# First q rows behind weights, two row blocks normalised together, last gates and Wo operands inside attention, two DMA queues at the end

## The chip, the cores and the metric

The kernel runs on one core of a Trainium2 chip. The metric is the device time of one execution in microseconds. The kernel before has a median of 1725.43 us over 3 runs (1724.54 to 1725.99). The core's engines run their own instruction streams in order and meet at semaphores: PE (TensorE, matrix products into PSUM), DVE (VectorE), ACT (ScalarE), POOL (GpSimd), and SP, which here only issues DMAs. Weight loads of PE are shown as PEld.

## The reference

The input x has 2048 rows of 512 numbers. Layer normalisation gives xn; attention with 32 heads of 16 numbers and a dense block with GELU both read it, and the second gates the first:

```python
x = A_x
xn = _layernorm(x, axis=-1)
# attention: qkv = xn @ wqkv; p = softmax(q k^T / 4); s = (p v) @ wo
s = _A_ref(xn, A_wqkv, A_wo)
# dense block: h = gelu(xn @ w1 + b1); h @ w2 + b2
g = _silu(_B_ref(xn, B_w1, B_b1, B_w2, B_b2))
return x + s * g
```

## The kernel before

Everything is float32. Products other than those of attention's probabilities are made from rounded halves: an operand is split into a part rounded to fp32r ("h", by ACT) and a remainder ("l", by DVE or POOL), and three matmuls (hh, hl, lh; `mm3`, L69) stand for one product.

*Stage 1 (L240 to L366)* walks over 16 blocks of 128 rows. For a block, `moments` (L267) takes the statistics on DVE, `rstd` (L272) makes one over the root with ACT's square root and four small DVE operations with a refinement, `norm` (L281) writes the normalised block and asks for a later block of x on SP, `turn` (L288) transposes it on PE and splits it (`split`, L65: ACT, then DVE), and `v_tile` (L296) multiplies it with the v weights, 12 matmuls. The v weights come in four pieces (`wv_r`), each rounded by ACT (L330) with its remainder by POOL (L331). SP asks for row blocks 0 and 1, then the four weight pieces, then row blocks 2 to 6. Twelve matmuls of an identity stand ahead of the first block (L325).

*Stage 2 (L476 to L507)* runs over 48 jobs: four make q and k rows for two groups of four heads each (`qk`), the other 44 are column blocks of the dense layer for a chunk of 512 rows (`up`, then `down` one job later). q and k go out to DRAM as halves (`qk_h`, `qk_l`) and come back in attention's layout: `load_k` (L96), `load_qs` (L127). The weights of a job (`raw`, two buffers) are asked for by `w_ahead` and split by `w_split` (ACT L236, POOL L237), both called in `behind`; on ACT the GELU of a job (L394, L395) stands behind the rounding of a later job's weights. Between the matmuls, `fill` puts score matmuls of attention's first pass (`s_one`, L158), each with a row maximum on DVE (L172). When one is due is set by a count of matmuls (slots) and by `LEAD`, how many are made in this stage (4 x 144), and `FILL0`, the slot from which they are spread (less 12).

*Stage 3 (L642 to L689)* is attention. 32 units (a group of four heads by a chunk of 512 queries) have 16 steps each; step n makes transposed scores on PE (`t_one`, L547), exp on ACT (L549) into one of three buffers, and the product with v one step behind (`pv_step`, L557). Other work is hung on a step and a place in it with `at(n, f, ..., pos=...)`: place 0 is behind the first of a step's four score matmuls and its exp, place 3, the usual one, behind the last. A unit's end is `o_move` (copy out of PSUM, denominators to `dr`, four row groups to `ot`), `o_den` (reciprocal, out to `den_d`, back as `dn`, spread over 16 partitions each) and `o_div` (L591, the division). When a chunk of queries has all its heads, its four row blocks get the product with Wo: `load_gx` (gate and x), `w_token` (operands split, L604, L605), `w_mul`, `w_out` (L622: multiply with the gate on DVE, add x, store). `gx` has four buffers, the split operands `oh` and `ol` three each.

*End (L690 to L706).* The last chunk's four row blocks (12 to 15; `T3`) are done by k instead of by block: `w_chunk(k)` splits 128 of the 512 columns for all four blocks, and the last column group alone waits for the last unit's division. The gates of these four blocks get their SiLU here; the others got theirs in stage 2.

The order of every engine is that of the program text. Every DMA from SP in the kernel before is issued in program order; a DMA issue also waits until the DMA that was issued eight before it has landed.

Of the kernel before, what the change touches and what calls it, by code (L numbers as in the profile page):

```python
# [10 lines left out]
AF = mybir.ActivationFunctionType  # L11
# [9 lines left out]
DH = 16  # L21
KT = D // P
NT = S // P
CH = 512
# [8 lines left out]
LEAD = 144  # L33
DONE = 490
KBACK = 71
FILL0 = 192
ORDER = {0: "TTTTV", 1: "TTTTSV", 2: "TTTSTSV", 3: "STTTSTSV", 4: "STTSTSVTS"}
KB = 3

# [2 lines left out]
def fused(ctx: ExitStack, tc: tile.TileContext, x, wqk, wv, wo, w1, b1, w2, b2, out):  # L42
    nc = tc.nc
# [13 lines left out]
    den_d = dpool.tile([NG * NCH, GH, CH], F32, name="den_d")  # L57
# [7 lines left out]
    def split(hi, lo, src):  # L65
        nc.scalar.activation(hi, src, AF.Copy)
        nc.vector.tensor_sub(lo, src, hi.bitcast(F32))  # L67
# [11 lines left out]
    NU = NG * NCH  # L79
# [23 lines left out]
    def k_zero(kt, i, eng):  # L103
        p, a = divmod(i, 2)
        eng.memset(kt[p][64 * a + 32:64 * a + 64].bitcast(F32), 0.0)

    def k_ones(kt):
        for p in range(2):
            for a in range(2):
                nc.sync.dma_start(kt[p][64 * a + 48:64 * a + 50].bitcast(F32), ones_d)  # L110
# [9 lines left out]
    def q_rows(qs, u):  # L120
        g, c = divmod(u, NCH)
        for a in range(2):
            for b, src in enumerate((qk_h, qk_l, qk_h)):
                r = 64 * a + DH * b
                nc.sync.dma_start(qs[a][r:r + DH].bitcast(F32), rows(src, g, 0, a, c * CH, CH))

    def load_qs(u):  # L127
        if u < LEAD // 16:
            QS[u] = qzs[u % 2]
            q_rows([QS[u][:, a] for a in range(2)], u)  # L130
        elif u < NU:
            QS[u] = qss[0][:, u % 2]
            q_rows([QS[u]] * 2, u)
# [106 lines left out]
    with ExitStack() as s1:  # L240
# [4 lines left out]
        def a_tile(shape):  # L245
            banks[0] += 1
            i = banks[0] % 6
            if i < 2:
                return ps_s.tile(list(shape), F32, name="ps")
            if i == 2:  # L250
                return ps_x.tile(list(shape), F32, name="ps")
            return ps_t.tile(list(shape), F32, name="pst")


        xs, xns = {}, {}

        def load_x(t):
            xs[t] = w1k.tile([P, D], F32, name="xt", bufs=7)
            nc.sync.dma_start(xs[t], x[t * P:(t + 1) * P, :])
# [7 lines left out]
        def moments(t):  # L267
            st = w1k.tile([P, 6], F32, name="st")
            nc.vector.bn_stats(st, xs[t])
            nc.vector.bn_aggr(mv[:, t, :], st)  # L270

        def rstd(t0, t1):  # L272
            v = ve[:, :, t0:t1]
            nc.vector.tensor_scalar(v[:, 0], mv[:, t0:t1, 1], EPS, None, op0=OP.add)
            nc.scalar.activation(v[:, 1], v[:, 0], AF.Sqrt)
            nc.vector.reciprocal(v[:, 2], v[:, 1])
            nc.vector.scalar_tensor_tensor(v[:, 3], v[:, 2], -0.5, v[:, 2], op0=OP.mult, op1=OP.mult)
            nc.vector.tensor_mul(v[:, 3], v[:, 3], v[:, 0])
            nc.vector.scalar_tensor_tensor(v[:, 4], v[:, 3], 1.5, v[:, 2], op0=OP.add, op1=OP.mult)

        def norm(t):  # L281
            xns[t] = w1k.tile([P, D], F32, name="xn", bufs=3)
            nc.vector.tensor_scalar(xns[t], xs.pop(t), mv[:, t, 0:1], ve[:, 4, t:t + 1],
                                    op0=OP.subtract, op1=OP.mult)
            if t + 7 < NT:
                load_x(t + 7)

        def turn(t):  # L288
            pt = a_tile((P, KT, P))
            xn = xns.pop(t)  # L290
            for k in range(KT):
                nc.tensor.transpose(pt[:, k, :], xn[:, k * P:(k + 1) * P], ident)  # L292
            c, ts = t // NCH, slice(t % NCH * P, t % NCH * P + P)
            split(xh[c][:, :, ts], xl[c][:, :, ts], pt)
# [11 lines left out]
        warm = wp.tile([1, 2], F32, name="warm")  # L306
# [18 lines left out]
        for _ in range(12):  # L325
            nc.tensor.matmul(pw[:, :P], ident, ident, start=True, stop=True)
        moments(0)
        rstd(0, 1)
        for k in range(KT):
            nc.scalar.activation(wv_h[:, k], wv_r[:, k], AF.Copy)  # L330
            nc.gpsimd.tensor_sub(wv_l[:, k], wv_r[:, k], wv_h[:, k].bitcast(F32))  # L331
        norm(0)
        moments(1)
        rstd(1, 2)
        norm(1)
        moments(2)
        turn(0)
        turn(1)
        moments(3)
        rstd(2, 4)  # L340
# [115 lines left out]
    def fill():  # L456
        prog["slot"] += 1
        n = prog["slot"]
        due = 4 * LEAD * (n + 12 - FILL0) // (slots - FILL0)
        held = n < prog["hold"] and not prog["credit"]  # L460
# [7 lines left out]
    def behind(i):  # L468
        w_ahead(i + 4)
        if i < NJ and jobs[i][0] == "m" and jobs[i][2] == 2 and silu:  # L470
            gate(2)
        if prev:
            down(prev.pop())
        w_split(i + 2)

    for i in range(NJ):  # L476
        if jobs[i][0] == "q":
            qk(i)
        else:
            up(i)  # L480
            behind(i)
            prev.append(i)
        if i == 0:
            k_ones(kts[0])
            load_k(0)
            load_qs(0)
        if i == 2:
            load_qs(1)
            for j in range(4):
                k_zero(kts[1], j, nc.vector)  # L490
        if i == 6:
            k_ones(kts[1])
            load_k(1)
        if i == NJ - FT:
            kts.append([slot(p, (P, S), F32R) for p in range(2)])
        if NJ - FT <= i < NJ - FT + 2:
            for j in range(2):
                k_zero(kts[2], 2 * (i - NJ + FT) + j, nc.gpsimd)
        if i == NJ - FT + 2:
            k_ones(kts[2])  # L500
            load_k(2)
        if i == NJ - 4:
            load_qt(0)
            load_mh(0)
            qss.append(slot(2, (P, 2, 2, CH), F32R))
            load_qs(LEAD // 16)
            load_qs(LEAD // 16 + 1)  # L507
# [6 lines left out]
    ot = [slot(6 + c, (P, KT, CH)) if c < 2 else kp.tile([P, KT, CH], F32, name=f"ot{c}") for c in range(NCH)]  # L514
# [16 lines left out]
    PT, PV, OS, DN, DR = {}, {}, {}, {}, {}  # L531
# [35 lines left out]
    def o_rows(u, j):  # L567
        g, c = divmod(u, NCH)
        r0 = 64 * (g % 2) + DH * j
        return slice(r0, r0 + DH), c, g // 2  # L570

    def o_move(u):
        DR[u] = wb.tile([P, GH * CH // P], F32, name="dr")
        nc.sync.dma_start(DR[u], OS[u][DH::32])
        for j in range(GH):
            r, c, k = o_rows(u, j)
            nc.sync.dma_start(ot[c][r, k], OS[u][32 * j:32 * j + DH])
        del OS[u]

    def o_den(u):  # L580
        dr = DR.pop(u)
        nc.vector.reciprocal(dr, dr)
        nc.sync.dma_start(den_d[u].rearrange("j (a i) -> (j a) i", i=GH * CH // P), dr)
        DN[u] = wb.tile([P, CH], F32, name="dn", bufs=1)
        for j in range(GH):
            nc.sync.dma_start(DN[u][o_rows(u, j)[0]], den_d[u, j:j + 1].to_broadcast([DH, CH]))

    def o_div(u, eng):
        g, c = divmod(u, NCH)
# [3 lines left out]
    GX, OTS, PW = {}, {}, {}  # L593

    def load_gx(t):
        GX[t] = wb.tile([P, 2, D], F32, name="gx", bufs=4)
        nc.sync.dma_start(GX[t][:, 0], g_d[t * P:(t + 1) * P, :])
        nc.sync.dma_start(GX[t][:, 1], x[t * P:(t + 1) * P, :])
# [14 lines left out]
    def w_chunk(k, lo):  # L613
        w_round([(t, k) for t in T3], ot[NCH - 1][:, k].rearrange("p (t s) -> p t s", s=P), lo)

    def w_mul(t, ks):
        if t not in PW:
            PW[t] = ps_m.tile([P, CH], F32, name="ps") if t == NT - 1 else s_tile()
        for k in ks:
            mm3(PW[t], OTS.pop((t, k)), (wo_h[:, k], wo_l[:, k]), k == 0, k == KT - 1)  # L620
# [9 lines left out]
    def at(n, f, *a, pos=3):  # L630
        todo.setdefault((n, pos), []).append((f, a))

    KS = tuple(range(KT))
    L = 16 * NU
# [7 lines left out]
    for u in range(NU):  # L642
        g, c = divmod(u, NCH)
# [12 lines left out]
    for c in range(NCH - 1):  # L656
        for i in range(NCH):
            t = c * NCH + i
# [3 lines left out]
            at(n + 2, w_mul, t, KS)  # L662
            at(n + 2, w_out, t, nc.gpsimd)
    T3 = range(NT - NCH, NT)
    for k in range(KT):
        at(40 + 16 * k, load_wo, k)
        at(48 + 16 * k, split_wo, k)
    for n in range(L + 1):
        ua, ka = divmod(n, 16)
        want = due(n) - sum(made)  # L670
        i = 0
        for op in ORDER[want]:
# [10 lines left out]
            else:  # L683
# [4 lines left out]
                    f(*args)  # L688
                i += 1  # L689
    o_move(NU - 1)  # L690
    for t in T3[:2]:
        load_gx(t)
    for k in KS[:-1]:
        w_chunk(k, nc.vector if k % 2 else nc.gpsimd)
    o_den(NU - 1)
    for t in T3[2:]:
        load_gx(t)
    for t in T3:
        w_mul(t, KS[:-1])
    for t in T3:  # L700
        nc.scalar.activation(GX[t][:, 0], GX[t][:, 0], AF.Silu)
    o_div(NU - 1, nc.vector)
    w_chunk(KT - 1, nc.vector)
    for i, t in enumerate(T3):
        w_mul(t, KS[-1:])
        w_out(t, nc.gpsimd if i % 2 == 0 else nc.vector)  # L706
# [33 lines left out]
```

## Time and profile before

| what | us |
|---|---|
| median of 3 runs | 1725.43 |
| profiled execution | 1724.45 |
| its span | 1722.7 |
| PE busy | 1692.6 |
| DVE busy | 1420.1 |
| ACT busy | 1258.7 |
| POOL busy | 316.9 |

The span runs from the first instruction to the last. Views that the next part uses: busy time in stretches of the span; instructions in order of time, merged where alike, as start, length, engine, line, operation, output and input, with the idle time of the engine before it and what ended that; and the chain of work that ended last, followed back from the end, whose rows give start, length and what it was. SPq and ACTq are instructions that only issue DMAs.

### The profile page before, as it was taken

Reading aid. Unit: us, or ns where it says so; the run is one execution under the profiler, and the core shown is the slowest. Engines: PE = TensorE matmul, PEld = TensorE weight load, DVE = VectorE, ACT = ScalarE, POOL = GpSimd, SP = SyncE. Lnnn points to the kernel's source line nnn. Section 1 sums busy time; section 2 is a strip of 40 time slices with the busy share of each in tenths; the row PEclk is TensorE's granted clock in tenths of the full one; section 3 lists DMA queues with packets and bytes.
Section 4 is the critical chain, followed back from the end, with each engine's and each line's share of the span. In section 5 each row is a group of like instructions: output and inputs, shape, how many; then the busy total and the mean of one; then the engine's idle time right before and its main releaser. Section 6 shows DMA issues by size and latency. Waiting matters only on the chain.

```text
span 1722.7 us, 27683 instructions
## 1 busy us (share of the span) xinstructions
PE 1692.6 (98%) x10136; PEld 899.2 (52%) x10136; DVE 1420.1 (82%) x2332; ACT 1258.7 (73%) x2381; POOL 316.9 (18%) x285
## 2 busy tenths in 40 slices
PE   8999999999999999999999999999999999999996
PEld 6878788787786333334443344444334333444443
DVE  6459998998998887888888888888888888887402
ACT  3432233233235999999999999999999999998772
POOL 2244144144352002000100100100100000001232
PEclk9999999999999999999999999999999999999998
DMA  4365422423351113211311311311131111112222
GB/s 153 104 150 109 144 79 81 141 83 103 123 122 56 26 24 64 57 29 28 66 36 28 65 28 38 54 39 27 42 59 26 23 39 27 30 26 78 73 96 94
DMA packets 74903, 115.03 MB, mean 67 GB/s; under 512 B 25268, under 2 KB 26292, under 8 KB 73208
## 3 DMA queue, kind: packets, MB, share of 16 engines
q1 hardware_dynamic: 71408, 100.92, 21.6%
q0 software_dynamic: 3360, 12.35, 4.0%
q8 instruction: 80, 1.31, 0.3%
q14 instruction: 55, 0.45, 0.1%
HBM read 82.78 MB, written 25.97 MB: 63 GB/s over the span
## 4 chain that ended last, share of the span: by engine, by line
PE 92%; DVE 3%; DMA 2%; ACT 1%; SPq 1%; issue 1%; POOL 0%; ACTq 0%; DVEq 0%; POOLq 0%
PE pv L557 29%; PE ps L170 26%; PE pst L547 11%; PE ps L72 11%; PE pst L72 9%; PE ps L547 4%; DVE mx L172 2%; PE pv L72 2%; ACT slot L549 1%; DVE hl L67 0%; DVE gt L436 0%; DMA kt<-qk_l 0%; DMA kt<-qk_h 0%; DMA wv_r<-in_wv 0%; PE ps L292 0%
## 5 line engine op out<-in xcount | busy, mean ns | idle before, releaser
L172 DVE TENSOR_REDUCE mx<-ps 128x1 f32<-128x512 f32 x2048 | 1312.0, 684 | 151.7 <-PE pst L547 71.7
L549 ACT ACTIVATE slot<-pst 128x512 f32<-128x512 f32 x1536 | 842.0, 614 | 48.1 <-PE pst L547 27.5
L557 PE MATMUL pv<-slot,vsb 128*32 128x512 f32 x4096 | 545.3, 605 | 1.6 <-ACT os L563 1.5
L547 PE MATMUL pst<-qt,kt 50*128 50x512 f32 x1152 | 366.9, 437 | 0.2 <-ACT slot L549 0.2
L170 PE MATMUL ps<-kt,slot 48*128 48x512 f32 x1024 | 366.6, 441 | 0.1
L549 ACT ACTIVATE slot<-ps 128x512 f32<-128x512 f32 x512 | 314.2, 614 | 22.0 <-PE ps L547 12.5
L170 PEld LDWEIGHTS ps<-kt,slot 48*128 48x128 f32 x1024 | 183.8, 184 | 274.6 <-DVE mx L172 251.6
L170 PE MATMUL ps<-kt,qz 128*128 128x512 f32 x512 | 203.4, 397 | 1.1 <-DVE mx L172 0.7
L547 PEld LDWEIGHTS pst<-qt,kt 50*128 50x128 f32 x1152 | 165.0, 185 | 68.0 <-ACT slot L549 44.5
L557 PEld LDWEIGHTS pv<-slot,vsb 128*32 128x32 f32 x4096 | 80.6, 108 | 176.7 <-issue 164.5
L547 PE MATMUL ps<-qt,kt 50*128 50x512 f32 x384 | 166.9, 435 | 0.0
L170 PE MATMUL ps<-slot,slot 48*128 48x512 f32 x448 | 162.0, 442 | 0.0
L72 PE MATMUL ps<-slot,wh 128*128 128x512 f32 x416 | 145.4, 397 | 3.3 <-ACT hg L395 3.3
L237 POOL TENSOR_TENSOR wl<-raw,wh 128x1024 fp32r<-128x1024 f32 x48 | 115.1, 2398 | 140.2 <-ACT wh L236 106.3
L170 PEld LDWEIGHTS ps<-slot,slot 48*128 48x128 f32 x448 | 81.4, 184 | 108.9 <-DVE mx L172 102.3
L236 ACT ACTIVATE wh<-raw 128x1024 fp32r<-128x1024 f32 x48 | 50.8, 1058 | 96.8 <-PE pv L72 87.6
L547 PE MATMUL pst<-qt,slot 50*128 50x512 f32 x384 | 117.5, 431 | 0.0
L185 POOL TENSOR_TENSOR nmh<-nm,nmh 128x16 fp32r<-128x16 f32 x32 | 7.0, 220 | 575.2 <-DVE nm L184 374.8
L170 PEld LDWEIGHTS ps<-kt,qz 128*128 128x128 f32 x512 | 96.3, 188 | 30.0 <-DVE mx L172 7.1
L394 ACT ACTIVATE hh<-ps,b_sb 128x512 fp32r<-128x512 f32 x40 | 27.5, 688 | 108.0 <-PE ps L72 108.0
L72 PEld LDWEIGHTS ps<-slot,wh 128*128 128x128 f32 x416 | 78.6, 189 | 21.7 <-ACT hg L395 3.7
L72 PE MATMUL ps<-slot,wl 128*128 128x512 f32 x208 | 82.4, 396 | 0.5 <-POOL wl L237 0.5
(132 smaller groups left out, 1483.3 us busy)
## 6 DMA issues: line engine op xcount, KB each, us to landing
raw<-in_w SPq DMA_DIRECT2D x88, 256.0 KB
qk_h<-hh SPq DMA_DIRECT2D x32, 256.0 KB
qk_l<-hl SPq DMA_DIRECT2D x32, 256.0 KB
qt<-qk_h SPq DMA_DIRECT2D x128, 64.0 KB
slot<-qk_h SPq DMA_DIRECT2D x92, 64.0 KB
xt<-in_x SPq DMA_DIRECT2D x16, 256.0 KB
g_d<-gt POOLq DMA_DIRECT2D x16, 256.0 KB, 2.9
qt<-qk_l SPq DMA_DIRECT2D x64, 64.0 KB
```

What stands on the lines that cost most here:

```text
L72: nc.tensor.matmul(ps, lhs[a], rhs[b], start=first and n == 0, stop=last and n == 2)
L170: nc.tensor.matmul(ps, q[r, p, qi * P:(qi + 1) * P], kts[g % KB][p][r, ki * CH:(ki + 1) * CH], start=True, stop=True)
L172: nc.vector.tensor_reduce(MX[u][:, 2 * p + a, qi, ki:ki + 1], ps, axis=AX.X, op=OP.max)
L185: nc.gpsimd.tensor_sub(NM[u][:, 1], nm, NM[u][:, 0].bitcast(F32))
L236: nc.scalar.activation(wh, W[i], AF.Copy)
L237: nc.gpsimd.tensor_sub(wl, W[i], wh.bitcast(F32))
L394: nc.scalar.activation(hh, ph, AF.Gelu_apprx_tanh, bias=b1_sb[:, f:f + 1])
L547: nc.tensor.matmul(ps, kts[g % KB][p][r, k * P:(k + 1) * P], QT[u][r, p, :], start=True, stop=True)
L549: nc.scalar.activation(PT[u, k][:, 2 * p + a, :], ps, AF.Exp, scale=SCALE)
L557: nc.tensor.matmul(PV[u][32 * j:32 * j + 32, :], vsb[:, k, h:h + 32], PT[u, k][:, j, :], start=(k == 0), stop=(k == NT - 1))
```

## The change

In stage 1 the statistics of row blocks 0 and 1 are taken first and get their roots together; both blocks are normalised before the v weights are split; a subtraction of one element on POOL reads block 1; block 0's transposition and split stand between the second and the third weight piece, and block 1's behind block 2's statistics. In stage 2 the q rows of units 0 and 1 are asked for two jobs and one job later than before, each behind the weights that the job asks for, and FILL0 goes from 192 to 200. At the end, the gate and x loads of blocks 12 to 14 and the splits of the first three column groups are hung on the last attention steps (508, 510, 512); the products with Wo go by column group; the last unit's four `ot` moves are issued by ACT, and of its four `dn` loads every second; three of the four gates come ahead of the last split, the load of block 15 behind the `dn` loads.

```diff
-FILL0 = 192
+FILL0 = 200
...
         moments(0)
-        rstd(0, 1)
+        moments(1)
+        rstd(0, 2)
+        norm(0)
+        norm(1)
+        nc.gpsimd.tensor_sub(warm[:, :1], xns[1][:1, :1], xns[1][:1, :1])
         for k in range(KT):
+            if k == 2:
+                turn(0)
             nc.scalar.activation(wv_h[:, k], wv_r[:, k], AF.Copy)
             nc.gpsimd.tensor_sub(wv_l[:, k], wv_r[:, k], wv_h[:, k].bitcast(F32))
-        norm(0)
-        moments(1)
-        rstd(1, 2)
-        norm(1)
         moments(2)
-        turn(0)
         turn(1)
...
             load_k(0)
-            load_qs(0)
+        if i in (2, 3):
+            load_qs(i - 2)
         if i == 2:
-            load_qs(1)
...
+        eng = nc.sync if u < NU - 1 else nc.scalar
         for j in range(GH):
             r, c, k = o_rows(u, j)
-            nc.sync.dma_start(ot[c][r, k], OS[u][32 * j:32 * j + DH])
+            eng.dma_start(ot[c][r, k], OS[u][32 * j:32 * j + DH])
...
         for j in range(GH):
-            nc.sync.dma_start(DN[u][o_rows(u, j)[0]], den_d[u, j:j + 1].to_broadcast([DH, CH]))
+            eng = nc.scalar if u == NU - 1 and j % 2 else nc.sync
+            eng.dma_start(DN[u][o_rows(u, j)[0]], den_d[u, j:j + 1].to_broadcast([DH, CH]))
...
+    for i, t in enumerate(T3[:-1]):
+        at(L - 4 + 2 * i, load_gx, t, pos=0)
+    for k in KS[:-1]:
+        at(L - 4 + 2 * k, w_chunk, k, nc.vector if k % 2 else nc.gpsimd, pos=0)
...
     o_move(NU - 1)
+    for k in KS[:-1]:
+        for t in T3:
+            w_mul(t, (k,))
     for t in T3[:2]:
-        load_gx(t)
-    for k in KS[:-1]:
-        w_chunk(k, nc.vector if k % 2 else nc.gpsimd)
+        nc.scalar.activation(GX[t][:, 0], GX[t][:, 0], AF.Silu)
     o_den(NU - 1)
-    for t in T3[2:]:
-        load_gx(t)
-    for t in T3:
-        w_mul(t, KS[:-1])
-    for t in T3:
-        nc.scalar.activation(GX[t][:, 0], GX[t][:, 0], AF.Silu)
+    load_gx(T3[3])
+    nc.scalar.activation(GX[T3[2]][:, 0], GX[T3[2]][:, 0], AF.Silu)
     o_div(NU - 1, nc.vector)
     w_chunk(KT - 1, nc.vector)
+    nc.scalar.activation(GX[T3[3]][:, 0], GX[T3[3]][:, 0], AF.Silu)
     for i, t in enumerate(T3):
         w_mul(t, KS[-1:])
```

## The prediction

> **What bounds the kernel now.** I read the page's busy line and chain first, then busy time by stretches, then the instructions in order of time at the three places that the change touches, with the chain of waits beside them.
>
> ```profile
> PE 1692.6 (98%) x10136; PEld 899.2 (52%) x10136; DVE 1420.1 (82%) x2332; ACT 1258.7 (73%) x2381; POOL 316.9 (18%) x285
> 0.00:19.00 19.00, 11.79 (x50) 10.09 (x51) 11.70 (x33) 5.57 (x11) 9.08 (x16) 0.82 0.64 199
> 114.00:170.00 56.00, 56.00 (x238) 45.24 (x237) 51.34 (x77) 15.49 (x21) 26.20 (x16) 0.97 0.48 110
> 170.00:545.00 375.00, 373.87 (x1611) 298.79 (x1610) 358.11 (x558) 118.63 (x159) 143.41 (x96) 1.00 0.34 104
> 545.00:1690.00 1145.00, 1143.09 (x7765) 461.34 (x7762) 942.85 (x1560) 1075.94 (x2121) 108.90 (x143) 1.00 0.20 44
> 1690.00:1723.00 33.00, 16.71 (x66) 10.71 (x64) 8.30 (x12) 4.84 (x7) 6.74 (x5) 0.77 0.33 112
> ```
>
> The columns of a stretch are its length, then busy us and count of PE, weight loads, DVE, ACT and POOL, then granted clock, DMA share and GB/s. From 114 to 1690 us TensorE rests 3 us in all: nothing there can be won without fewer matmuls, and the change removes none. What can be won is TensorE's idle time at the start (7.2 us of 19), the hole before 114, and the end (16.3 us of 33), with the half clock that follows a hole. These are the change's three places. The profiled execution took 1724.45 us, its span 1722.7 and 1.75 around it; the shown runs have a median of 1725.43, 0.98 above it. I sum against 1724.45 and shift the result by 0.98.
>
> **Start: two row blocks normalised together.** Rows in order of time (start, length), and one of the chain:
>
> ```profile
> 4.43 0.15 DVE L274 TENSOR_SCALAR ve<-mv 128x1 f32<-128x1 f32 x1
> 5.25 0.16 DVE L278 TENSOR_TENSOR ve<-ve 128x1 f32<-128x1 f32 x1
> 5.63 0.55 DVE L283 TENSOR_SCALAR xn<-xt,mv,ve 128x512 f32<-128x512 f32 x1
> 6.10 0.69 DVE L269 BATCH_NORM_STATS2 st<-xt 128x6 f32<-128x512 f32 x1
> 6.49 4.93 POOL L331 TENSOR_TENSOR wv_l<-wv_r,wv_h 128x512 fp32r<-128x512 f32 x4 [4.03 <-ACT wv_h L330]
> 9.38 0.16 DVE L276 RECIPROCAL ve<-ve 128x1 f32<-128x1 f32 x1 [2.19 <-ACT ve L275]
> 10.25 1.18 DVE L278 TENSOR_TENSOR ve<-ve 128x1 f32<-128x1 f32 x1
> 11.66 0.55 DVE L283 TENSOR_SCALAR xn<-xt,mv,ve 128x512 f32<-128x512 f32 x1
> 13.38 5.00 PE pst L72 x12
> ```
>
> Block 1's square root stands on ACT behind four weight conversions (DVE idles 2.19 us for it), then its small products wait for POOL (1.18 us for what took 0.16 at 5.25), so block 1 is normalised at 11.66 and the first product of the v stage runs 13.38 to 18.38, at half clock after TensorE's pause. Changed: block 1's statistics come before the shared root. From 6.10 to the next L274 was 0.94, so L274 moves from 4.43 to 5.37 (block 1's rows need to have landed by 4.4; they had no wait at 6.10), the norms follow 1.20 later at 6.57 and 0.46 after that, at 7.03 to 7.58. POOL's added one-element subtraction reads block 1 and holds POOL until then, and with it what is queued behind, the remainders that the first product waits for: these four (4.93) run about 7.75 to 12.7 instead of 6.49 to 11.42. ACT interleaves block 0's split between the second and third conversion; the product starts near 8.5, and its last group needs the fourth remainder: end near 13.2. Block 2's small products again wait for POOL, to 12.7, and its norm ends near 13.8, so the regular train that began at 18.4 begins at 13.9 to 14.0: **gain 4.4**. Bounds: if the product can only run whole and at half clock behind POOL (12.7 + 5.00), 0.7; if POOL held nobody, 5.5. I take the instruction order's value, as the product's groups need the remainders one at a time.
>
> [...]
>
> **Middle: q rows behind weights.** Timeline, chain and one stretch:
>
> ```profile
> 99.38 6.65 DMA kt<-qk_l
> 106.04 0.35 SPq L223 DMA_DIRECT2D raw<-in_w  x1
> 106.04 3.36 DMA raw<-in_w
> 108.06 0.39 PE L72 MATMUL pv<-wh,hl 128*128 128x512 f32 x1
> 109.51 1.06 ACT L236 ACTIVATE wh<-raw 128x1024 fp32r<-128x1024 f32 x1 [8.04 <-DMA raw<-in_w]
> 111.78 0.74 PE L72 MATMUL ps<-slot,wh 128*128 128x512 f32 x2 [3.32 <-ACT hg L395]
> 113.06 0.49 PE L72 MATMUL ps<-slot,wl 128*128 128x512 f32 x1 [0.55 <-POOL wl L237]
> 1706.00:1708.00 2.00, 0.00 (x0) 0.00 (x0) 0.00 (x0) 0.81 (x2) 0.00 (x0) 0.50 0.95 358
> ```
>
> TensorE waits for a GELU (L395) that stands on ACT behind the conversion L236 of a weight pair that landed at 109.40. That pair was asked for at 106.04, behind six q-row loads (384 KB); with them gone in front it is asked for right after the last k rows, about 101. It cannot land before these (106.03), since one ring serves all, and behind them its 512 KB need 1.4 us at 358 GB/s, or 1.9 as its share of the 3.36 us in which 896 KB came: 107.5, bounds 106.03 and 107.95. Conversion, GELU, TensorE and remainder all follow **1.9 earlier** (1.4 to 3.4). The clock of 0.97 over 56 us is 1.7 us of lost clock after this hole; what is left of it (1.5 us, then 0.8 before the remainder) is short beside the 3.3 us that lost the clock, so I count **1.4** of the 1.7 (bounds 0, 1.7). The q rows themselves then land some 1.5 us later than now, and the first score matmul is also moved eight fill slots later (FILL0 200; eight matmuls, 1.9 us): it finds them there. The 576 scores of this stage then have 1.9 us less room; DVE, which reduces them, has 16.9 us free in 375. I charge **-0.3** (bounds 0 and -1.9). The second q load waits behind a further weight pair, and its scores come 64 later.
>
> [...]
>
> **End: gates and Wo operands earlier, two queues.**
>
> ```profile
> 1648.59 0.38 SPq L583 DMA_DIRECT2D den_d<-dr  x1
> 1650.40 1.71 SPq L586 DMA_DIRECT2D dn<-den_d  x4
> 1679.25 0.18 PEld L547 LDWEIGHTS pst<-qt,kt 50*128 50x128 f32 x1 [0.31 <-ACT slot L549]
> 1690.14 0.63 ACT L604 ACTIVATE oh<-ot 128x512 fp32r<-128x512 f32 x1 [0.42 <-PE ps L72]
> 1692.27 0.69 DVE L565 COPY os<-pv 128x512 f32<-128x512 f32 x1 [1.21 <-PE pv L557]
> 1692.45 0.33 SPq L626 DMA_DIRECT2D out<-gx  x1
> 1692.99 0.63 SPq L574 DMA_DIRECT2D dr<-os  x1
> 1694.92 0.25 DVE L582 RECIPROCAL dr<-dr 128x16 f32<-128x16 f32 x1 [0.73 <-DMA dr<-os]
> 1696.77 0.43 SPq L598 DMA_DIRECT2D gx<-in_x  x1
> 1698.24 3.54 DMA den_d<-dr
> 1701.77 0.40 PE L72 MATMUL ps<-wo_h,ol 128*128 128x512 f32 x1
> 1701.84 1.72 SPq L586 DMA_DIRECT2D dn<-den_d  x4
> 1705.18 0.69 DVE L591 TENSOR_TENSOR ot<-ot,dn 64x512 f32<-64x512 f32 x1 [10.01 <-DMA dn<-den_d]
> 1708.36 0.61 ACT L604 ACTIVATE oh<-ot 128x512 fp32r<-128x512 f32 x1
> 1711.48 1.28 POOL L625 TENSOR_TENSOR gx<-gx 128x512 f32<-128x512 f32 x1 [16.14 <-DVE gx L624]
> 1715.28 0.69 DVE L625 TENSOR_TENSOR gx<-gx 128x512 f32<-128x512 f32 x1
> ```
>
> The path is the last unit's denominators: out of the copy os, to dr, inverted, to memory, back as dn, the division at 1705.18, then L604 at 1708.36, held 2.5 us by gates that came last, then twelve matmuls. In the order of the changed program:
> Two of the three early L604 (0.63) stand between exps for which TensorE already waits (0.31 on one load): attention ends **1.2 later**, os at 1694.2. The third stands behind the last exps. Their remainders go to POOL and DVE, which have room: POOL's first two wait on ACT alone, and the add queued behind the first is due 3 us later.
> On SP, dr now stands behind the last output store and block 14's two gate loads (0.43 each and gaps): issue 1695.0, not 1692.99; its data come behind 512 KB, so it lands near 1697.5 (before: 1.9 after issue; bounds 1696.9 and 1698.5). The four ot moves leave SP for ACT, off the path; behind them on ACT stand only the first two gates. Blocks 12 and 13 load on SP between the output stores of the last steps, each behind a store that waits for POOL's add; nothing else on SP is due there, since the last unit's own loads are long in. Inversion 0.3; den_d goes at once (1697.9, where four gate loads held it to 1698.24) and lands as the earlier one did, 1.8 to 1.9 later, not 3.54: 1699.8. Two dn issues on each queue instead of four on one (0.43 each): issued by 1700.7 instead of within 1.72, and division follows 1.6 behind the last, as now (1703.56 to 1705.18): 1702.3. ACT is free for its two by then: four ot issues to 1696.7, a table load and two gates (under 3 us) to 1699.5. L604 comes right behind, with the last gate moved behind it and the one before it done while dn is in flight: ends 1703.7 where it ended 1708.97. **Gain 5.3.**
> TensorE's 36 earlier products, without their POOL waits, end near 1701.7 and don't bind. Behind L604 the DVE chain to the last store (7.0 us now, twelve matmuls at half clock) hardly shortens at full clock: its two DVE adds (0.69), which now fall just behind POOL's adds of 1.28, would then come up against them and wait, as the small product did at 10.25. I take 0.1 off, bounds 0 and 1.5. ACT issues no DMA now, so its price is bounded by SP's 0.33 and 0.63 and, for a loss, 1.5: the term is 5.4 with bounds 2.5 and 7.
>
> Sum: 4.4 + 1.9 + 1.4 - 0.3 + 5.4 = 12.8. 1724.45 - 12.8 = 1711.65; as a median, **1712.6**.
>
> **Rivals.**
> The weights land no sooner, because k rows or the bytes ahead set it: the middle gives nothing, 1715.6. For it: 6.65 us for one k row group. Against: 384 KB do go from in front. Chance 0.12.
> The denominators' chain isn't shorter: dr behind the loads and ACT's dear issues eat the gain, leaving 1.5 of 5.4: 1716.5. For it: den_d's 3.54 us behind loads shows that such queueing costs. Against: two loads instead of four. 0.15.
> Slower: the reductions become the pace from 114 to 545, as all scores are due closer together. DVE has 16.9 us free, 15 after the change; over some 500 scores that is 0.03 us each. From a handover dearer by more than that it decides; at 0.06, 30 - 15 = 15 us: 1727.6. Against: DVE keeps up now with TensorE idle 1.1 us of 375. 0.05.
> The earlier start and the filled hole are taken back by something with its own time, and the end breaks even: 1725. Against: in the long stretches TensorE is never short of data. 0.05.
>
> **Numbers.** Forecast 0.63: 1709 to 1715. The range goes to the middle rivals and the bounds: 1708.8 to 1718.0. No change within 0.2% (3.5 us, about what a measurement of this kernel can tell): 0.05; slower 0.05; faster 0.90, all other cases.
>
> **What would show it.** Block 1's norm near 7, the train of twelve matmuls of 2.81 us from about 14.4; a weight pair asked for before the first q rows, the hole of TensorE near 104 under 2.5 us and no half clock after it; den_d and its dn within 2 us; L604 right behind the division. Wrong would be: a wait of TensorE on kt or q rows at the first score, idle time before pst L547 growing over many steps, dr landing over 3 us after its issue, or the fill stretch longer than 431 us.

## The result, and the profile after

| | before | after |
|---|---|---|
| median of 6 runs each, side by side | 1726.05 us | 1714.12 us |
| lowest and highest | 1724.54 to 1727.18 | 1712.46 to 1716.21 |
| profiled execution | 1724.45 | 1712.75 |
| its span | 1722.7 | 1710.9 |

The ratio is 0.9931, 95% interval 0.9918 to 0.9944: 11.9 us faster, where 12.8 from the profiled execution's time was forecast. The profiled time fell by 11.7.

First the stretches of the span after the change (columns as in the prediction):

```profile
0.00:19.00 19.00, 15.44 (x68) 11.78 (x69) 12.35 (x36) 7.54 (x15) 9.68 (x17) 1.00 0.64 220
114.00:170.00 56.00, 56.00 (x245) 45.52 (x244) 50.58 (x77) 17.27 (x23) 24.75 (x14) 1.00 0.48 107
170.00:545.00 375.00, 373.81 (x1622) 295.50 (x1624) 361.01 (x563) 122.21 (x170) 141.85 (x95) 1.00 0.34 105
```

TensorE rests 3.6 of the first 19 us (7.2 before), and at full clock (0.82 before). From 114 to 170 us the clock is 1.00 (0.97 before). From 170 to 545 DVE has 14.0 us free, and TensorE still rests 1.2, so the slower rival (reductions as the pace) did not come.

The start, instructions in order of time:

```profile
5.06 0.17 DVE L274 TENSOR_SCALAR ve<-mv 128x2 f32<-128x2 f32 x1
6.29 1.00 DVE L283 TENSOR_SCALAR xn<-xt,mv,ve 128x512 f32<-128x512 f32 x2
7.60 5.00 POOL L337 TENSOR_TENSOR wv_l<-wv_r,wv_h 128x512 fp32r<-128x512 f32 x4
8.49 0.51 PE L72 MATMUL pst<-wv_h,slot 128*128 128x512 f32 x1 [0.49 <-ACT slot L66]
11.99 0.63 DVE L274 TENSOR_SCALAR ve<-mv 128x2 f32<-128x2 f32 x1
13.68 0.55 DVE L283 TENSOR_SCALAR xn<-xt,mv,ve 128x512 f32<-128x512 f32 x1
14.69 0.48 PE L72 MATMUL pst<-wv_h,slot 128*128 128x512 f32 x1
```

Both norms are done by 7.29. The first product starts at 8.49 and runs beside POOL's remainders, group by group. L274, the first small operation for block 2's root, takes 0.63 at 11.99, where the one at 5.06 took 0.17, and ends as POOL does, near 12.6. The first matmul of the regular train (the stage's products from the second block on) is at 14.69. In the timeline of the kernel before it is this one, 3.9 us later:

```profile
18.58 0.48 PE L72 MATMUL pst<-wv_h,slot 128*128 128x512 f32 x1
```

The middle, in order of time:

```profile
96.22 0.36 SPq L222 DMA_DIRECT2D raw<-in_w  x1
98.00 0.34 SPq L125 DMA_DIRECT2D qz<-qk_h  x1
104.45 1.06 ACT L236 ACTIVATE wh<-raw 128x1024 fp32r<-128x1024 f32 x1 [6.68 <-DMA raw<-in_w]
106.72 0.73 PE L72 MATMUL ps<-slot,wh 128*128 128x512 f32 x2 [1.97 <-ACT hg L396]
108.00 0.50 PE L72 MATMUL ps<-slot,wl 128*128 128x512 f32 x1 [0.55 <-POOL wl L237]
```

The weights now go ahead of the q rows (qz), directly behind the last k rows (95.21). Their conversion starts at 104.45 instead of 109.51; of these 5.1 us, 3.8 are the lead from the start, which the last copy of v shows (L302, 62.88 for 66.67). The hole, TensorE's wait for the GELU behind that conversion and then for the remainder, is 1.97 + 0.55 us instead of 3.32 + 0.55, and no half clock follows it.

The end, in order of time:

```profile
1686.62 0.69 DVE L566 COPY os<-pv 128x512 f32<-128x512 f32 x1 [1.27 <-PE pv L558]
1688.10 0.63 SPq L575 DMA_DIRECT2D dr<-os  x1
1691.72 0.25 DVE L584 RECIPROCAL dr<-dr 128x16 f32<-128x16 f32 x1 [4.41 <-DMA dr<-os]
1692.01 0.31 SPq L585 DMA_DIRECT2D den_d<-dr  x1
1693.40 0.79 SPq L589 DMA_DIRECT2D dn<-den_d  x2
1696.28 0.69 DVE L594 TENSOR_TENSOR ot<-ot,dn 64x512 f32<-64x512 f32 x1 [4.30 <-DMA dn<-den_d]
1697.05 0.63 ACT L607 ACTIVATE oh<-ot 128x512 fp32r<-128x512 f32 x1 [2.11 <-DVE ot L594]
1699.82 1.29 POOL L628 TENSOR_TENSOR gx<-gx 128x512 f32<-128x512 f32 x1 [11.87 <-DVE gx L627]
1700.47 1.20 DVE L628 TENSOR_TENSOR gx<-gx 128x512 f32<-128x512 f32 x1
```

From the copy os to the division are 9.66 us where there were 12.91, and the last split (L607, L604 before) comes 0.77 behind the division's start where it came 3.18 behind: it waits for no gate any more. dr takes 3.62 from its issue to the reciprocal (1.93 before), den_d lands in 1.4 instead of 3.5. The DVE add (L628 at 1700.47), 0.69 before, now meets POOL's and takes 1.20.

### The profile page after: what moved, and what is told of

It is laid out like the page before. It is cut to its first block, busy times and chain, and to the rows that moved or that the text cites. A ratio compares the mean times of both kernels' runs of the same rounds, so it can differ in the third digit from the quotient of the medians.

```text
span 1710.9 us, 27677 instructions
## 1 busy us (share of the span) xinstructions
PE 1688.9 (99%) x10136; PEld 895.0 (52%) x10136; DVE 1419.6 (83%) x2327; ACT 1258.7 (74%) x2380; POOL 317.6 (19%) x286
## 4 chain that ended last, share of the span: by engine, by line
PE 89%; DVE 3%; DMA 3%; issue 2%; ACT 1%; POOL 1%; SPq 1%; ACTq 0%; DVEq 0%; POOLq 0%
PE pv L558 29%; PE ps L170 27%; PE pst L548 11%; PE ps L72 9%; PE pst L72 7%; PE ps L548 4%; PE pv L72 2%; DVE mx L172 1%; ACT slot L550 1%; DMA qk_l<-hl 1%; DMA raw<-in_w 1%; DVE gt L437 0%; POOL wl L237 0%; DVE hl L67 0%; DMA xt<-in_x 0%
## 5 line engine op out<-in xcount | busy, mean ns | idle before, releaser
L397 POOL TENSOR_TENSOR hl<-hg,hh 128x512 fp32r<-128x512 f32 x44 | 56.9, 1293 | 148.1 <-ACT hg L396 81.2
```

The costliest lines, as they stand in the source:

```text
L397: nc.gpsimd.tensor_sub(hl, hg, hh.bitcast(F32))
```

## Experiments

Most undo or add one thing in the changed kernel; "the theory" and "the rival" are those of the expectation above each result. A clock window is there a piece of half clock, 3.41 us in the kernel before (113.69 to 117.10). The intervals of the ratios to the kernel before are about 0.0015 to either side, some 2.5 us, so single microseconds are read from marks in the profiles.

**The start undone**

```diff
-        moments(1)
-        rstd(0, 2)
-        norm(0)
-        norm(1)
+        rstd(0, 1)
...
+        norm(0)
+        moments(1)
+        rstd(1, 2)
+        norm(1)
```

> The changed kernel with only its start undone (one root for each of the first blocks, weight conversions ahead of them, no hold on POOL). Theory: the start is worth 4.1 us, the lead with which the regular train of twelve matmuls begins (14.69 against 18.82 us), and it is carried to the end: about 1718.2 us, the train again from 18.7 or so with TensorE's clock low before it, everything after it about 4 us later, with the hole before the first scores unchanged (restart wait of about 2 us). Rival: the loads of weights and k rows have a time of their own, so that a later start is waited for in any case: the hole shrinks by as much and the time stays near 1714 to 1715.

Median 1719.38 us, 0.9961 of before (0.9946 to 0.9975); the changed kernel run again, in another series, had 1714.88 (below): 4.5 us more. The train's first matmul and the hole, in order of time:

```profile
17.95 0.48 PE L72 MATMUL pst<-wv_h,slot 128*128 128x512 f32 x1
110.94 0.94 PE L72 MATMUL ps<-slot,wh 128*128 128x512 f32 x2 [3.04 <-ACT hg L395]
```

The granted clock over the first 19 us is 0.82 again, and the hole didn't shrink by the delay: 3.04 us. So the theory holds in that the start's lead goes through to the end. Its size is another matter. The 18.82 us of the expectation is a row of the chain, where the changed kernel's train stands at 14.94, not 14.69; so the lead over the kernel before is 3.9 us, not 4.1, and over this run, whose train begins at 17.95, 3.3. The rest of the 4.5 is inside the intervals.

**Without the hold on POOL**

```diff
-        nc.gpsimd.tensor_sub(warm[:, :1], xns[1][:1, :1], xns[1][:1, :1])
```

> The changed kernel without the one-element subtraction that holds POOL until block 1 is normalised. [...] Rival: the hold is what the start's gain hangs on, because block 1's norm is pushed behind more than one remainder (each 1.25 us): first product later than 9.5 and train later than 15, time 1714.5 to 1717.

Median 1716.97 us, 0.9946 (0.9931 to 0.9961). In order of time, and then the stretch of the start:

```profile
6.43 1.98 DVE L283 TENSOR_SCALAR xn<-xt,mv,ve 128x512 f32<-128x512 f32 x2
14.20 0.66 PE L292 MATMUL pst<-ident,xn 128*128 128x128 f32 x4 [1.37 <-DVE xn L283]
14.62 0.68 PE L72 MATMUL pst<-wv_h,slot 128*128 128x512 f32 x1
```

```profile
0.00:19.00 19.00, 13.86 (x60) 10.91 (x61) 13.02 (x37) 6.68 (x13) 9.47 (x16) 0.91 0.68 222
```

Beside POOL's first remainder (from 6.86) block 1's norm ends at 8.41 instead of 7.29, and block 2's norm, which ends at 14.15, is only 0.08 sooner, so the train begins at 14.62 (14.69 in the changed kernel) after a longer wait of TensorE, 1.37 us, and its first matmul takes 0.68 us for 0.48, at a granted clock of 0.86 from 14 to 15 us and 0.50 behind that. The rival's sign came (2.1 us more than the changed kernel run again), by another way than the rival said. Whether the hold is worth this stays open: two of the eleven profiles with the new start and the hold lost the clock at the same place (0.91 over the first 19 us).

**q rows ahead of the weights again**

```diff
             load_k(0)
+            load_qs(0)
-        if i in (2, 3):
-            load_qs(i - 2)
         if i == 2:
+            load_qs(1)
```

> The changed kernel with the first q rows asked for in their old place, ahead of the weight pairs (fill start kept at slot 200). Theory: the pair lands again 3.4 us after it is asked for, TensorE's wait for the GELU is again 3.3 us instead of 1.97, and the clock is lost for a window after it (granted 0.97 over the stretch from 114 to 170, shifted): 1.4 + 1.7 = 3.1 us slower than the changed kernel, about 1717.2. Rival: the earlier start alone moved the weights, or the eight fill slots did, and the order of the q rows gives nothing: 1714, hole of 2 us, clock 1.00.

Median 1716.93 us, 0.9950 (0.9934 to 0.9967), the hole in order of time, then the stretch around it:

```profile
108.76 0.73 PE L72 MATMUL ps<-slot,wh 128*128 128x512 f32 x2 [4.03 <-ACT hg L396]
```

```profile
100.00:126.00 26.00, 21.43 (x86) 16.77 (x85) 11.54 (x17) 6.86 (x9) 10.89 (x6) 0.93 0.61 146
```

The hole is 4.03 us, against 1.97 to 3.11 in the eight profiles that have the new order and no other edit at this place: the order of the q rows does shorten it, and the rival falls, though this side has one profile. That the time is only 2 us above the changed kernel's, which the intervals don't separate, is explained by the next profiles.

**The end undone**

```diff
-    for k in KS[:-1]:
-        at(L - 4 + 2 * k, w_chunk, k, nc.vector if k % 2 else nc.gpsimd, pos=0)
...
-        eng = nc.sync if u < NU - 1 else nc.scalar
...
     o_den(NU - 1)
+    for t in T3[2:]:
+        load_gx(t)
+    for t in T3:
+        w_mul(t, KS[:-1])
```

> The changed kernel with its end undone (gates and Wo operands behind the last move, all moves on one queue). Theory: the end is worth 5.1 us: attention ends 1.0 us sooner, and the chain from the last copy to the last store is 6.1 us longer: about 1719.2, den_d landing in about 3.5 us instead of 1.4 and TensorE at half clock for the last twelve matmuls. Rival: the lead is eaten since the three early conversions cost attention more than the gates' move brings: 1714 to 1716.

Median of 9 runs 1721.85 us, 0.9971 (0.9961 to 0.9981): 7.0 above the changed kernel run again. The stretch around the hole, whose code is the changed kernel's:

```profile
100.00:126.00 26.00, 22.65 (x85) 17.58 (x85) 11.15 (x17) 6.86 (x9) 10.89 (x6) 0.87 0.57 144
```

In order of time, the hole and the end:

```profile
107.64 0.74 PE L72 MATMUL ps<-slot,wh 128*128 128x512 f32 x2 [2.82 <-ACT hg L396]
...
1689.28 0.69 DVE L566 COPY os<-pv 128x512 f32<-128x512 f32 x1 [1.21 <-PE pv L558]
1702.43 0.69 DVE L592 TENSOR_TENSOR ot<-ot,dn 64x512 f32<-64x512 f32 x1 [10.25 <-DMA dn<-den_d]
1705.60 0.63 ACT L702 ACTIVATE gx<-gx 128x512 f32<-128x512 f32 x1 [1.69 <-DMA gx<-g_d]
1706.13 0.61 ACT L605 ACTIVATE oh<-ot 128x512 fp32r<-128x512 f32 x1
```

From the copy os to the end of the span are 31.2 us (1720.5 - 1689.28) against 24.3 in the changed kernel (1710.9 - 1686.62): 6.9, less the 1.0 that attention's steps lose: 5.9, near the theory's 5.1. The largest piece is the last split behind the last gate, whose load was asked for late: 3.7 behind the division's start. The rival falls. The surprise is the middle: the same code as the changed kernel's has a hole of 2.82 us and a clock of 0.87 over 26 us, (1 - 0.87) x 26 = 3.4 us of lost clock, where the changed kernel's profile had none.

**The changed kernel again**

No edit.

> The changed kernel unaltered, beside the three others on the same chip, for a second profile of it. Theory: the hole before the first scores is not the same in every execution: its length follows the landing of the last k rows and the weights behind them, and the clock is lost there for none, one or two windows; mean clock between 0.994 and 0.998 from run to run with up to 3.7 us between runs, and a hole of 2.4 us or more in this profile, so that the 1.97 us of the first one was on the lucky side. Rival: the first profile is typical: hole 2.0, full clock after it, and the longer holes of the variants were their own doing.

Median 1714.88 us, 0.9935 (0.9919 to 0.9950), runs 1714.57 to 1716.57. The hole, then the stretches of the start and around the hole:

```profile
109.04 0.74 PE L72 MATMUL ps<-slot,wh 128*128 128x512 f32 x2 [2.72 <-ACT hg L396]
```

```profile
0.00:19.00 19.00, 14.07 (x59) 10.67 (x60) 12.87 (x36) 6.45 (x13) 9.66 (x17) 0.91 0.63 216
100.00:126.00 26.00, 22.74 (x92) 17.80 (x91) 11.13 (x17) 6.86 (x9) 11.64 (x7) 0.93 0.62 152
```

The theory holds, with 2.0 us between these runs and 3.75 between those of the first series. Identical code, yet the hole is 2.72 us instead of 1.97, and a stretch of half clock is lost in it and another near 14 us. The profiles of the same middle side by side (hole is TensorE's first wait, then its second; lost clock is (1 - clock) x 26 us from 100 to 126):

| profile | hole | clock | hole and lost clock |
|---|---|---|---|
| changed kernel, first | 1.97 + 0.55 | 1.00 | 2.5 us |
| changed kernel, again | 2.72 + 0.54 | 0.93 | 5.1 |
| end undone | 2.82 + 0.53 | 0.87 | 6.7 |
| gates early (below) | 2.39 + 0.55 | 0.93 | 4.8 |
| dn on one queue (below) | 3.11 + 0.33 | 0.93 | 5.3 |
| splits on DVE (below) | 2.98 + 0.55 | 0.93 | 5.4 |
| before | 3.32 + 0.55 | 0.93 | 5.7 |
| q rows ahead again | 4.03 + 0.54 | 0.93 | 6.4 |

The first six have a mean of 5.0: 0.7 below the kernel before, 1.4 below the q rows' old place, each of which has one profile here. The profiles without the new start and without the hold, whose middle is the same, have 5.2 each. The first profile was the lucky one.

**TensorE kept busy in the hole**

```diff
             down(prev.pop())
+        if i == 4:
+            pz = s_tile()
+            for _ in range(8):
+                nc.tensor.matmul(pz[:, :P], ident, ident, start=True, stop=True)
         w_split(i + 2)
```

> The changed kernel with eight small matmuls of the identity (128 columns each, result unused) in TensorE's queue between the last product before the hole and the first one after it. Theory: the hole of about 2 to 3 us stays as long, but TensorE is busy for most of it, so that no clock window is lost there: the GELU after the hole comes 5.5 us after the one held in it, where 6.6 to 7.7 were seen with one or two lost windows; 1 to 2 us below the changed kernel run beside it in the median. Rival: the clock is lost by the weights' late remainder or by chance, and not by idleness in the hole: same number of lost windows, no gain.

Median 1714.56 us, 0.9929 (0.9914 to 0.9945), runs 1712.39 to 1715.77. TensorE's only wait there in order of time, then the stretch:

```profile
107.72 0.50 PE L72 MATMUL ps<-slot,wl 128*128 128x512 f32 x1 [0.56 <-POOL wl L237]
```

```profile
100.00:126.00 26.00, 25.44 (x119) 20.71 (x118) 14.88 (x22) 7.92 (x10) 12.97 (x7) 1.00 0.68 164
```

Full clock, as the theory had it, and the next GELU 5.45 us after the one in the hole. But the first profile of the changed kernel kept its clock too, and a median 0.3 lower is no difference: inconclusive for the time.

**Late weight pair by halves, first try**

```diff
         HS[i] = (hh, hl)
+        if i == 2:
+            w_split(3, nc.vector)
...
-        w_split(i + 2)
+        if i != 1:
+            w_split(i + 2)
```

> The changed kernel with the late weight pair converted by halves, its remainder on DVE, and the GELU of the job before ahead of it on ACT. Theory: the weights' landing is the floor and what stands behind it on ACT and POOL (conversion 1.06, GELU 1.25, remainder 2.36) is the rest of the hole: TensorE restarts within 0.6 us of the landing and waits under 0.8 more for the remainder, 2.0 us sooner than in the changed kernel's profile. Since the changed kernel loses none, one or two clock windows of 3.4 us there (granted 1.00 over 100 to 126 in its own profile, half clock from 108.4 to 115.0 in the profile of the kernel with the old end), it also keeps full clock in every run: 2 to 4 us faster in the median, and runs closer together. Rival: TensorE waits for q rows or k rows at the first scores instead, so that the wait only moves: no gain.

Median 1715.76 us, 0.9932 (0.9917 to 0.9947). The pair taken (fourth job) had landed long before; the late one is the sixth job's. So the hole stands, and the run tells nothing of the theory, but gives one more hole that cost the clock (0.93):

```profile
107.37 1.22 PE L72 MATMUL ps<-slot,wh 128*128 128x512 f32 x2 [2.29 <-ACT hg L402]
```

**The right pair, and the one after it**

```diff
+    LATE = (5, 6)
...
+            for s in (0, 1) if i in LATE else (slice(0, 2),):
+                nc.scalar.activation(wh[:, s], W[i][:, s], AF.Copy)
+                eng = nc.vector if i in LATE else nc.gpsimd
+                eng.tensor_sub(wl[:, s], W[i][:, s], wh[:, s].bitcast(F32))
...
         HS[i] = (hh, hl)
+        if i + 1 in LATE:
+            w_split(i + 1)
```

> The changed kernel with the late weight pair (the sixth job's) and the one after it converted by halves, their remainders on DVE, and the GELU of the job before ahead of them on ACT. Theory: the landing of the pair is the floor, and conversion 1.06, GELU 1.25 and the remainder's 2.36 on POOL are what is left of the hole; TensorE then waits at most 0.4 us for a half conversion and 0.5 for a half remainder where it waited 1.97 + 0.55 (2.4 to 3.1 + 0.5 in the other profiles of the same code): 1.5 to 2.5 us, and no clock window of 3.4 us is lost there (1.7 us each): 2 to 4 us below the changed kernel run beside it, mean clock 0.997 or more in all runs. Rival: the first scores or the pair after it make TensorE wait as long: the wait moves, under 1 us gained.

Median 1713.45 us, 0.9922 (0.9904 to 0.9940); the run beside it of the changed kernel had 1714.88. The only idle time of TensorE in the timeline from 94 to 118, and what DVE did before it:

```profile
110.21 1.90 DVE L240 TENSOR_TENSOR wl<-raw,wh 128x512 fp32r<-128x512 f32 x2 [1.42 <-ACT wh L238]
112.77 0.50 PE L170 MATMUL ps<-kt,qz 128*128 128x512 f32 x1 [2.16 <-DVE mx L172]
```

The hole is gone, but the second pair's remainder (1.90, beside a POOL operation) now stands on DVE ahead of the first score maxima, TensorE waits 2.16 us for one, and the clock over 100 to 126 is 0.93 again. Theory right on the hole, rival right on the moved wait: 1.4 us, not separated by the intervals. The first pair alone wasn't tried.

**Block 14's gate loads one step earlier**

```diff
-        at(L - 4 + 2 * i, load_gx, t, pos=0)
+        at(L - 4 + 2 * i - (i == 2), load_gx, t, pos=0)
```

> The changed kernel with block 14's two gate loads one step earlier, ahead of the last output store, so that dr stands behind that store alone. Theory: dr landed 3.60 us after its issue because 512 KB were in front of it; it is now issued near 1687.2 instead of 1688.10 (on the clock of the changed kernel's profile) and lands within 2.4, so den_d is issued 2 us sooner; but ACT, which has four ot issues, a table load and two gates before its share of dn, is free only at 1692.4, so the division comes only 1.0 us sooner: 1 us faster than the changed kernel, with dn's two queues now at different times. Rival: dr's landing has nothing to do with the loads ahead of it (four engines' worth of ot moves beside it set it): still over 3 us, no gain.

Median 1713.01 us, 0.9918 (0.9902 to 0.9935). In order of time:

```profile
1688.76 0.69 DVE L566 COPY os<-pv 128x512 f32<-128x512 f32 x1 [1.27 <-PE pv L558]
1689.48 0.63 SPq L575 DMA_DIRECT2D dr<-os  x1
1691.66 0.25 DVE L584 RECIPROCAL dr<-dr 128x16 f32<-128x16 f32 x1 [2.21 <-DMA dr<-os]
1693.59 0.38 ACTq L589 DMA_DIRECT2D dn<-den_d  x1
1693.92 0.62 ACT L702 ACTIVATE gx<-gx 128x512 f32<-128x512 f32 x1
1696.28 0.69 DVE L594 TENSOR_TENSOR ot<-ot,dn 64x512 f32<-64x512 f32 x1 [4.36 <-DMA dn<-den_d]
```

dr takes 2.18 us to the reciprocal instead of 3.62, and from the copy to the division are 7.52 instead of 9.66: 2.1 us, and not the 1.0 to which ACT was to limit it. In the program's order ACT's first issue of dn stands behind two gates, but it went out at 1693.59, before the second of them began (1693.92): that gate did not hold the issue behind it. The rival falls.

**dn on one queue**

```diff
-            eng = nc.scalar if u == NU - 1 and j % 2 else nc.sync
+            eng = nc.sync
```

> The changed kernel with the four last dn issues on SP alone. Theory: two more issues of 0.43 us stand in front of the last one, the division follows about 2.2 us behind that one as it does now: 0.85 us slower than the changed kernel (about 1 part in 2000). Rival: the landing is what takes the time, and the four issues overlap with it: no difference in the distance from den_d's issue to the division (4.27 us now).

Median 1715.42 us, 0.9935 (0.9921 to 0.9950). In order of time:

```profile
1694.40 0.31 SPq L585 DMA_DIRECT2D den_d<-dr  x1
1699.13 0.69 DVE L594 TENSOR_TENSOR ot<-ot,dn 64x512 f32<-64x512 f32 x1 [4.76 <-DMA dn<-den_d]
```

From den_d's issue to the division are 4.73 us against 4.27: the second queue is worth 0.46, half of the theory's 0.85. The four issues take 1.71 us (1695.80 to 1697.51) instead of 0.87 (1693.40 to 1694.27), but the division follows 1.62 behind the last of them instead of 2.01.

**Early splits on DVE**

```diff
-        nc.scalar.activation(oh[:, :n], src, AF.Copy)
+        if hi is None:
+            nc.scalar.activation(oh[:, :n], src, AF.Copy)
+        else:
+            hi.tensor_copy(oh[:, :n], src)
```

The three early column groups pass DVE as `hi`.

> The changed kernel with the three early conversions of Wo operands on DVE instead of ACT. Theory: attention's last steps lost 1.04 us to two conversions of 0.62 between exps that TensorE waits for (0.84 us of idle at a load of pst, twice); on DVE, which is idle there, they delay nobody: the idle goes, attention ends 1.0 us sooner, time 1.0 us lower. Rival: the 0.84 us come from the order of the steps (stores, loads, gates), not from ACT: idle stays.

Median 1714.86 us, 0.9929 (0.9914 to 0.9944). In order of time, the last stores and one weight load:

```profile
1675.92 0.34 SPq L632 DMA_DIRECT2D out<-gx  x1
1676.21 0.20 PEld L548 LDWEIGHTS pst<-qt,kt 50*128 50x128 f32 x2 [0.84 <-ACT slot L550]
1682.91 0.34 SPq L632 DMA_DIRECT2D out<-gx  x1
1689.96 0.34 SPq L632 DMA_DIRECT2D out<-gx  x1
```

Between the last three stores lie 6.99 and 7.05 us; in the changed kernel 7.56 and 7.52 (stores at 1671.65, 1679.21, 1686.73). So the steps are 1.04 us shorter, the theory's size, though the wait of 0.84 stands there as before, now for an exp and not for the split. The median doesn't show it (1714.86 against 1714.88); this profile, the slowest of the four runs, lost the clock at the start (0.91 over 19 us) as well as in the hole.

**Three edits together: a version that beats both**

Gates early, early splits on DVE, and the two pairs by halves, as above.

> The changed kernel with the three edits together: block 14's gate loads one step earlier (2.1 us from the copy os to the division, measured), the early conversions on DVE (1.04 us of attention's last steps, measured), and the late weight pairs by halves with their remainders on DVE (2 to 4 us by theory). Theory: the three lie at different times and add up: 5 to 7 us below the changed kernel run beside it, about 0.996 of its time. Rival: DVE, given conversions and remainders, delays the score reductions or the copy os, and takes back half or more: under 3 us.

Median 1711.13 us, runs 1709.58 to 1711.15, 0.9909 of before (0.9893 to 0.9924). Beside it the changed kernel ran 1714.57 to 1716.57: 3.75 us lower in the median, every run below every run. Less than the theory's 5 to 7, above the rival's 3: the pairs brought 1.4 alone, not 2 to 4.

## Why the prediction was right

**Start, 4.4 forecast, 3.9 measured.** Norms at 6.29 to 7.29 (6.57 to 7.58 forecast), remainders from 7.60 to 12.60 (7.75 to 12.7), first product from 8.49: the order of events was as written. The missing 0.4 are in block 2's norm, which ends at 14.23 and not 13.8: the first of the small operations (L274 at 11.99) ended with POOL, at 12.62 and 12.60, where the forecast had only the later ones wait. At the last copy of v the lead is 3.8 us; in the second profile of the same code, which lost the clock near 14 us, it is 2.1.

**Middle, 1.9 + 1.4 - 0.3 = 3.0 forecast.** In the first profile 1.35 of hole and all of the 1.7 of clock came, 3.0 in sum with the scores' later start at no visible cost: between the last copy of v and the last GELU of stage 2 the lead grows by 3.1. Over the six profiles with this code it grows by 1.1 in the mean. The mechanism is right (with the q rows ahead again, the hole is 4.03), but two steps were mis-sized. The first is the landing, "107.5, bounds 106.03 and 107.95", which was worked out from one execution (its page has one queue for all of SP's transfers, q1 with 100.92 MB, and in its chain the k rows land at 106.03, ahead of the pair, at 109.40): the changed kernel's chain has the pair landing 7.28 us after its last issue, at 104.35, which is 108.1 on the clock of the kernel before (3.8 us of lead added), and 108.5 to 109.2 in the other five; the kernel before has 109.4. So the pair comes 0.2 to 1.3 sooner, and not 1.9. The second is "what is left of it is short beside the 3.3 us that lost the clock, so I count 1.4": holes from 2.29 to 3.11 us lost about 1.8 us of clock each, one of 2.82 lost 3.4, and the 1.97 alone lost none.

The same kernel lost no clock around the hole in one profile and 1.8 us ((1 - 0.93) x 26) in the other. The lost clock is near one or two halves of 3.41 us, the length of a piece of half clock: 1.8 and 3.4 us. A wait of 2.29 us was enough for it.

The traces also show where the luck lies. Half clock came in pieces of 3.41 us (113.69 to 117.10 before, 110.05 to 113.46 in the second profile) or twice that (11.29 to 18.11 before). If one counts on in such pieces from each profile's own changes of the clock, every piece around the hole in which TensorE rests 1.93 us or more is followed by half clock, in all profiles, and no piece at full clock with 1.82 or less is. In the first profile a boundary at 105.82 cuts the 2.52 us of waits into 1.07 and 1.45; in the second, 2.68 us fall into one piece. This is an estimate, as the ends of matmuls are modelled, and no rule for other places: near 14 us, among matmuls that wait one by one, a piece with 1.44 us of rest lost the clock. Why the profile with the end undone lost a second piece stays open.

**End, 5.4 forecast, 5.1 in the first profile (5.9 against the end undone).** From the copy os to the end of the span are 24.3 us instead of 30.4 (1722.7 - 1692.27). Attention's last steps lose 1.04 (1.2 forecast). dr is issued 0.8 behind the end of the copy, as forecast, but takes 3.6 us where 2.5 was taken and 3.5 was the bound: the prediction had named a landing over 3 us as a sign of being wrong, and this step was. With the loads out of its way dr takes 2.2. den_d landed in 1.38, where 1.8 to 1.9 was taken, which gave 0.4 back. The second dn queue is worth 0.46, not the 0.86 of two issues. The split comes right behind the division, as forecast, and this is the main gain: 3.18 to 0.77 us. The DVE adds meet POOL's (1.20 and 1.26 for 0.69), as forecast, so the tail behind the last split is about 0.5 shorter, inside the bounds 0 and 1.5.

**Rivals.** The one that the weights land no sooner failed in the first profile, but comes nearer to most executions than the forecast does: the middle gives about 1. The denominators' chain is shorter, reductions are not the pace, and nothing was taken back.

**The sum, and luck.** Four marks in the traces add up to the whole; in brackets the lead over the kernel before:

| mark | before | first profile | second profile |
|---|---|---|---|
| last copy of v (L302) | 66.67 | 62.88 (3.8) | 64.54 (2.1) |
| last GELU of stage 2 | 537.89 | 531.01 (6.9) | 534.72 (3.2) |
| last unit's copy os | 1692.27 | 1686.62 (5.7) | 1690.47 (1.8) |
| end of the span | 1722.7 | 1710.9 (11.8) | 1714.8 (7.9) |

The first profile's terms are 3.8 + 3.1 - 1.2 + 6.1; the second's are 2.1 + 1.0 - 1.4 + 6.1, all rounded. The end is the same in both. That the first came within about 1 us of the forecast's 12.8 is luck: it kept its clock at the start and in the hole. The medians, 11.9 apart, agree with the forecast for another reason. The forecast was summed against one execution of the kernel before, and the 1724.45 us of that execution lie below all 31 other runs of that kernel on record, whose four medians are 1726.05 to 1727.09. Over the six profiles the start gives 3.1 in the mean and the middle 1.1, and the end, less attention's loss, 4.8 in the two profiles of the unaltered changed kernel: 9.0 against that execution, and 10.6 to 11.6 against the medians; what is left to 11.9 is inside the intervals.

Undone one at a time, start, q rows and end cost 4.5, 2.1 and 7.0 us in the medians, 13.6 together, where the change brings 12; each of these is only known to some 2.5 us.

## What to carry to other kernels

Count a hole's idle time and the clock lost after it apart, and the second as a chance: here, by the estimate above, it hung on where a boundary of the 3.41 us pieces fell in the hole. Ask several profiles of the same code, before and after the change, before a single one is believed. On the path at the end, look at what stands ahead of a small transfer on its queue and its engine: the gate loads ahead of dr and the gate ahead of the last split each cost more than 2 us (2.1 and 2.4), while splitting the issues over two queues brought 0.46. Moving work to an idle engine pays only if nothing due stands behind it there: with the pair's remainder on DVE (1.90), TensorE waited 2.16 us for a score maximum.

## What the runs showed of the hardware that was not expected

Two profiles of one kernel differ by 0.75 us in a wait for the same transfers, and one has half clock in two places where the other has none. With the gate loads earlier, ACT issued a DMA (1693.59) before an activation ahead of it in the program had begun (1693.92). A DVE operation on 128x2 elements beside POOL's remainder took 0.63 us (0.17 at 5.06, without it) and ended with it, near 12.6; without the hold on POOL, two 128x512 norms took 1.98 us instead of 1.00. Why these took longer, no trace here shows.
